# The opening of a fused attention and expert kernel in another order: first inverse ahead of weight conversion, two inverses alternating, chunk 2's scores in earlier slots

## The chip, the cores and the metric

The kernel runs on one core of one Trainium2 chip. The metric is the time of one execution on the device, in microseconds (us). The version before took 1119.66 us (median of 3 runs, 1117.63 to 1121.74).

## The reference: what is computed

Three layers, one behind the other, on 4 batches of 768 positions. The first is a recurrence over positions with a 40 x 40 state for each of 8 heads, the second a gated projection, the third a choice of one expert of 8 for each token.

```python
for t in range(S):                       # attention: B=4, H=8, S=768, D=40
    y[:, :, t] = r_t @ state
    Sa = state @ a_t
    state = state * w_t - outer(Sa, b_t) + outer(v_t, k_t)
...
x = ((x @ w_a) * (x @ w_b)) @ w_out      # 3072 x 320 -> 1536 -> 320
...
expert = argmax(x @ w_gate)              # 8 experts
out = gate * (relu(x @ w1[expert]) @ w2[expert])
```

## The kernel before

The recurrence is worked in 12 chunks of 64 positions. Inside a chunk it becomes matrix products, once a small triangular system is solved. For each chunk the kernel

- loads the decays w, the rows a, b, k and r, and scans w along the chunk (L558 to L563, VectorE), scales b and k by the scan (L601, VectorE) and a by w (L574, GpSimd);
- spreads a and r over the heads (`ablk`, `rblk`, L578, ScalarE), takes the scores as matrix products (L611) and copies them out of PSUM (L619); GpSimd masks them (L621), and SyncE sends them to a scratch tensor `nd` in DRAM (L628);
- reloads them as `m` (L677, L679), one system of 32 x 32 in each partition, and inverts it in `tinv` on VectorE: 31 steps, each one multiplication (L686, `tmp<-m,xt`) and one subtraction (L692, `xt<-xt,tmp`). `xt` starts as the identity, which is loaded (L680). A step reads what the step before wrote;
- sends `xt` to DRAM (`td`, L703) and back in another layout (`s`, L707, L708), transposes and multiplies it there (`forward`: L725, L729, L736, L748, L752), and uses it with the values (`vn`, `pu`, L810) and the state (L821 to L913) for the chunk's result.

`phase1` runs over the chunks c = 0 to 11, each in 24 slots. Tables say what each slot issues: `FIRST` for c = 0 and 1, `STEADY` and `LAST` for the others. With chunk c run matrix products of the gated projection of chunk c-1 (L1071), parts of the inverse of chunk c+1, and the scans, spreads and scores of chunk c+2.

In c = 0 and 1 the kernel also turns the projection weights from 32-bit words of two bit fields into pairs of an upper and a lower TensorE operand: `split64`, of 30 pieces and 4 steps a piece that `conv.take` hands out. A piece takes four VectorE operations on the raw words (L420, L424, L433, L435; tiles `c_f`, `c_s`), some three to six on ScalarE (L422, L430, L432, L443) and two or three on GpSimd (L438, L440, L445). The raw words come by DMA (L972 to L975), some pieces ahead. Pieces are named by their part of the weights: `raw_0_2` is the one with L443 on ScalarE and L440 on GpSimd, where GpSimd must have ended before ScalarE's L443. The tiles c_f have 3 buffers, c_s 2.

Ahead of the loop stands the opening: scans for chunks 0 and 1, scores of both, chunk 0's inverse, a first part of chunk 1's, and the first conversion steps. `mix` lays lists of operations beside one another in even proportion. The order of operations on TensorE, VectorE, ScalarE and GpSimd is the order of the code; each of these engines goes through it strictly. SyncE only issues DMAs; their order is made by the scheduler from the code's order and each DMA's needs. SyncE too takes them one after another, and one that must wait holds those behind it.

Touched by the change are `phase1` (the opening and the loop's use of the tables), the table `FIRST`, the scores, `tinv`, a new `load_x`, and the loading ahead in `split64`.

Of the kernel before, what the change touches and what calls it, by code (L numbers as in the profile page):

```python
# [8 lines left out]
F32 = mybir.dt.float32  # L9
# [13 lines left out]
R = C // 2  # L23
# [108 lines left out]

def phase1(tc, I, cst, drm, psA, psM, ident, hT, mk_ident, wo, xs, span, tiny, down):
    nc = tc.nc
# [3 lines left out]
    A = Attention(tc, I, att, mid, cst, drm, psA, ident, dv, ot, span)  # L138
    A.sink, M.pc = M, A.p2

    def run(fs):
        for f in fs:
            f()

    conv = M.weight_steps()
# [27 lines left out]
    for pr in range(2):  # L173
        A.scale_a(0, pr)
        A.spread_a(0, pr)
    A.ones()
    M.ahead()
    for b in range(B):
        A.scores(0, b)
# [4 lines left out]
        A.rows(0, b)  # L184
    tinv = A.tinv(0)
    for pr in range(2):
        A.vload(0, pr)
        A.load_r(0, pr)
    for pr in range(2):
        A.scale_a(1, pr)  # L190
        A.spread_a(1, pr)
    n0, n1, n2, n3 = FIRST["conv0"]
    run(conv.take(n0))
    for b in range(B):
        A.scores(1, b)
    for b in range(B):
# [2 lines left out]
    uh = [view(M.p2.tile([128, 2, 256], F32, tag="uh", name=f"m1_{h}")) for h in range(2)]  # L199
    xt = M.p2.tile([128, 2, 256], F32, tag="wo", name="xt1", bufs=1)  # L200
    t1 = A.tinv(1, (uh, view(xt)))
    run(conv.take(n1))
    A.relayout(0)
    A.relayout(1)
    mix(tinv, conv.take(n2))
    A.load_w(2)
    for h in range(2):
        A.load_bk(2, h)
    lead = FIRST["lead"]
    mix(t1[:lead], [lambda: A.forward((0, 0))] + conv.take(n3))  # L210
    t1 = t1[lead:]
    over = [A.spans(0, [t[:120, 0:L // 2].bitcast(F32) for t in sp])]
    units, tinv = [], t1
    for c in range(NCH + 1):
# [149 lines left out]
    if not down:  # L364
# [25 lines left out]
        [], [("stage4", 0, 1)], [("stage2v", 2, 3)], [],  # L390
        [("stage5", 0, 1), ("stage3", 2, 3)], [], [("px", 1, 0)],
        [("stage4", 2, 3)], [], [], [("stage5", 2, 3)], [], [], [], []],
    "conv0": [8, 6, 10, 8], "lead": 16, "early": 13, "extra": [10, 17], "ones": [2, 14],
    "conv": [
# [6 lines left out]
    "load_a": [19, 21], "r00": [2, 3, 4], "r1": [8, 9, 10], "score": [15, 16, 17, 18], "row": [16, 17, 22, 23],  # L401
    "tinv": [4, 4, 4, 4, 4, 4, 4, 4, 4, 4, 4, 2, 0, 0, 0, 0, 0, 0, 0, 0, 0, 0, 0, 0], "relayout": 14, "load_w": 15,
    "span": 18, "scan": [21, 22, 22, 23, 23],
}

# [54 lines left out]
class Attention:  # L460
# [144 lines left out]
    def scores(self, c, b):  # L605
        nc = self.nc
        st = self.st[c]
        ps = self.ps.tile([128, 512], F32, tag="pa", name=f"s1p{c}_{b}")
        for g in range(3):
            n = 3 if g < 2 else 2  # L610
            nc.tensor.matmul(  # L611
                ps[:2 * C, 3 * g * C:(3 * g + n) * C], self.bk5(c, b, g),
                self.ablk[b // 2][:, b % 2, g, 0:n, 0:C], start=True, stop=True)
        pr = b // 2
        if b % 2 == 0:
            st["s1"][pr] = self.p2.tile([128, 2, 8, C], F32, tag=f"s1_{pr}", name=f"s1_{c}_{pr}")
        s1p = st["s1"][pr]
        s1 = s1p[:, b % 2]
        nc.scalar.copy(s1, ps.rearrange("p (h t) -> p h t", t=C))  # L619
        v = s1[vrows(b)]  # L620
        nc.gpsimd.affine_select(  # L621
            out=v, in_=v, pattern=[[0, 8], [1, C]], base=0,
            channel_multiplier=-1, compare_op=ALU.is_gt, fill=0.0)
        def send():
            for k in range(2):
                for x in range(2):
                    s = 16 * pr + 8 * x
                    nc.sync.dma_start(  # L628
                        st["nd"][k, s:s + 8].rearrange("s j t -> j s t"),
                        s1p[urow(x, R * k), x, :, R * k:R * k + R])  # L630
# [19 lines left out]
    def relayout(self, c):  # L650
# [6 lines left out]
        for k, p0, p1, g, q0 in (  # L657
            (0, 0, 120, 0, 0), (0, 120, 128, 1, 0), (1, 0, 112, 1, 8), (1, 112, 128, 2, 0),
            (2, 0, 64, 2, 16), (2, 64, 128, 2, 16)):
            nc.sync.dma_start(gp[p0:p1, k, :, 0:C], v[q0:q0 + p1 - p0, :, g, :])  # L660

    def tinv(self, c, room=None):


        nc = self.nc
        st = self.st[c]
        if room:
            m, xt = room
        else:
            t = self.p1.tile([128, R, R], F32, tag="m", name=f"m{c}")  # L670
            m = [t[:, R // 2 * h:R // 2 * h + R // 2] for h in range(2)]
            xt = self.p1.tile([128, R // 2, R], F32, tag="xt", name=f"xt{c}")
        for k in range(2):
            for q in range(2):
                p = slice(64 * k + 32 * q, 64 * k + 32 * q + 32)
                for h in range(2 if room else 0):
                    nc.sync.dma_start(m[h][p], st["nd"][k, :, R // 2 * h:R // 2 * h + R // 2])  # L677
                if not room:
                    nc.sync.dma_start(t[p], st["nd"][k])  # L679
        nc.sync.dma_start(xt, self.I["one"].rearrange("p (i t) -> p i t", t=R))  # L680

        def mul(s, box):
            n, rows = R - 1 - s, s // 2 + 1
            tmp = self.p2.tile([128, 136], F32, tag="tmp", name=f"tmp{c}_{s}")[:, :rows * n]
            box.append(tmp.rearrange("p (i t) -> p i t", t=n))
            nc.vector.tensor_tensor(  # L686
                box[0], m[2 * s // R][:, s % (R // 2):s % (R // 2) + 1, s + 1:].to_broadcast([128, rows, n]),
                xt[:, :rows, s:s + 1].to_broadcast([128, rows, n]), op=ALU.mult)

        def sub(s, box):  # L690
            rows = s // 2 + 1
            nc.vector.tensor_tensor(  # L692
                xt[:, :rows, s + 1:], xt[:, :rows, s + 1:], box[0], op=ALU.subtract)
# [224 lines left out]
class MoeUp:  # L918
# [31 lines left out]
    def weight_steps(self):  # L950
# [10 lines left out]
        def load(j):  # L961
            if j in raws or j >= len(pieces):
                return
            f, q, k = pieces[j]
            f2 = slice(2 * f, 2 * f + 2 * n)
            pool, tag = (self.p2, ("xh", "xl")[j % 2]) if self.early else (self.pc, "raw")
            if self.extra and not self.early and j % 2:
                raw = raws[j] = self.extra[j // 2 % 2]
            else:
                raw = raws[j] = pool.tile([128, 2 * n], I32, tag=tag, name=f"raw{f}_{q}_{k}")  # L970
            if k < 2:
                nc.sync.dma_start(raw, ws[q][128 * k:128 * k + 128, f2])  # L972
            else:
                nc.sync.dma_start(raw[lo], ws[0][256:320, f2])
                nc.sync.dma_start(raw[hi], ws[1][256:320, f2])  # L975

        self.ahead = lambda: [load(j) for j in range(3)]

        def step(j):
            f, q, k = pieces[j]  # L980
            fs = slice(f, f + n)
            for d in range(3 if self.early or self.extra else 2):
                load(j + d)
            raw = raws[j]
# [849 lines left out]
```

## Time and profile before

| what | us |
| --- | --- |
| median of 3 runs | 1119.66 |
| the profiled execution, its own time | 1117.87 |
| its span, from the first to the last instruction | 1115.7 |
| TensorE busy in the span | 984.3 (88%) |
| VectorE busy | 698.4 (63%) |
| ScalarE busy | 590.9 (53%) |
| GpSimd busy | 428.6 (38%) |

The profiled execution lies 1.79 us under the median; 2.2 us of its time lie outside the span. Its mean granted TensorE clock is 0.942 of full speed.

The profile names the engines PE (matrix products) and PEld (weight loads) of TensorE, DVE (VectorE), ACT (ScalarE), POOL (GpSimd) and SP (SyncE; SPq is its queue of DMA issues). The opening takes the stretch from 0 to about 62 us of the span, the loop's c = 0 that from 62 to 135, c = 1 from 135 to 202, c = 2 from 202 to about 253.

### The profile page before, as it was taken

The page shows a single profiled execution, that of the slowest core. Times are in us where ns is not written, and L with a number is a line of the kernel's source. Part 1 is how long each engine was busy: PE and PEld are TensorE (multiplying, and loading weights), DVE is VectorE, ACT ScalarE, POOL GpSimd, SP SyncE. Part 2 cuts the span into 40 slices and gives each one's busy share as a digit, 9 for nine tenths or more (in the row PEclk, how much of TensorE's full clock was granted, in tenths as well). Part 3 has the DMA queues.
Part 4 walks back from the last instruction along what each step waited for, and adds up shares of the span by engine and source line. Part 5 has one row for each costly group of instructions (what it writes and reads, how often), then busy time and mean ns, then how long its engine had stood idle before and what let it go on. Part 6 is the DMA issues. An engine that isn't in the chain of part 4 may idle for free.

```text
span 1115.7 us, 27103 instructions
## 1 busy us (share of the span) xinstructions
PE 984.3 (88%) x10402; PEld 941.8 (84%) x10402; DVE 698.4 (63%) x1843; ACT 590.9 (53%) x1373; POOL 428.6 (38%) x469
## 2 busy tenths in 40 slices
PE   4054587999999999999999999999999999999994
PEld 4054487999898989899899999999998899999994
DVE  7889689686886969697875821336667732222230
ACT  5357867566666666566665553323334354444430
POOL 4326555233423334343232123002224467666641
PEclk9556689899999999999999999979999999999997
DMA  8553343476758576575756124715567264444500
GB/s 206 154 154 87 100 127 100 129 152 161 144 153 175 139 169 150 134 159 148 148 139 137 55 75 113 225 60 179 165 181 235 92 216 141 142 147 141 161 17 16
DMA packets 200663, 154.10 MB, mean 138 GB/s; under 512 B 107269, under 2 KB 182630, under 8 KB 200524
## 3 DMA queue, kind: packets, MB, share of 16 engines
q1 hardware_dynamic: 187196, 132.91, 45.2%
q0 software_dynamic: 9808, 15.76, 5.9%
q10 hardware_dynamic: 3520, 3.61, 1.2%
q8 instruction: 84, 1.38, 0.5%
q14 instruction: 55, 0.45, 0.2%
HBM read 103.66 MB, written 44.60 MB: 133 GB/s over the span
## 4 chain that ended last, share of the span: by engine, by line
PE 58%; DVE 18%; DMA 8%; issue 5%; ACT 4%; POOL 3%; SPq 1%; POOLq 0%; DVEq 0%; ACTq 0%
PE pm L1071 18%; PE py L1208 9%; PE dn L1517 6%; PE u L1497 6%; DVE tmp L686 3%; DVE xt L692 3%; PE s1p L611 3%; PE p L871 2%; DMA out<-y,ids 2%; PE pp L855 1%; PE py L895 1%; PE ta L729 1%; PE px L800 1%; PE tb L748 1%; DVE suf L559 1%
## 5 line engine op out<-in xcount | busy, mean ns | idle before, releaser
L878 POOL TENSOR_SCALAR_AFFINE_SELECT s<-s 64x512 f32<-64x512 f32 x96 | 75.9, 790 | 169.0 <-ACT s L876 164.8
L686 DVE TENSOR_TENSOR tmp<-m,xt 128x126 f32<-128x126 f32 (+22 forms) x372 | 116.4, 313 | 33.1 <-DMA xt<-in_one 14.6
L1071 PE MATMUL pm<-xl,wh 128*128 128x256 f32 x576 | 129.3, 306 | 1.3 <-ACT ua L1074 1.1
L1500 DVE SCALAR_TENSOR_TENSOR hl<-u,hh 128x384 fp32r<-128x384 f32 (+5 forms) x72 | 41.5, 580 | 139.8 <-ACT hh L1499 139.8
L1083 DVE TENSOR_TENSOR uh<-pm,ua 128x256 f32<-128x256 f32 x144 | 60.2, 418 | 105.4 <-PE pm L1071 58.5
L692 DVE TENSOR_TENSOR xt<-xt,tmp 128x126 f32<-128x126 f32 (+22 forms) x372 | 115.9, 311 | 8.6
L1071 PE MATMUL pm<-xh,wl 128*128 128x256 f32 x576 | 116.6, 284 | 0.0
L1071 PE MATMUL pm<-xh,wh 128*128 128x256 f32 x576 | 116.4, 284 | 0.0
L1208 PE MATMUL py<-wh,hl 128*128 128x328 f32 x288 | 91.2, 317 | 2.5 <-DVE hl L1198 2.5
L1208 PE MATMUL py<-wl,hh 128*128 128x328 f32 x288 | 92.2, 320 | 0.6 <-DVE wl L1179 0.6
L1071 PEld LDWEIGHTS pm<-xl,wh 128*128 128x128 f32 x576 | 89.0, 192 | 4.4 <-ACT ua L1074 1.7
L1208 PE MATMUL py<-wh,hh 128*128 128x328 f32 x288 | 90.8, 315 | 0.0
L1071 PEld LDWEIGHTS pm<-xh,wh 128*128 128x128 f32 x576 | 90.5, 193 | 0.0
L1071 PEld LDWEIGHTS pm<-xh,wl 128*128 128x128 f32 x576 | 90.1, 192 | 0.0
L1071 PE MATMUL pm<-xh,w 128*128 128x256 f32 x288 | 82.0, 285 | 0.0
L1071 PE MATMUL pm<-xl,w 128*128 128x256 f32 x288 | 81.9, 284 | 0.0
L1261 POOL DMA_INDIRECT xs<-xr,si x24 | 28.0, 1166 | 137.8 <-DVE acc L1256 88.0
L729 PE MATMUL ta<-t,s 32*32 32x32 f32 x768 | 23.8, 202 | 61.7 <-DVE t L725 58.0
L729 PEld LDWEIGHTS ta<-t,s 32*32 32x32 f32 x768 | 18.8, 116 | 67.3 <-ACT wh L432 32.5
L1050 POOL TENSOR_TENSOR xl<-xf,xh 128x384 fp32r<-128x384 f32 x24 | 24.8, 1034 | 131.5 <-ACT xh L1049 131.5
L1517 PE MATMUL dn<-l,hh 128*128 128x320 f32 (+3 forms) x240 | 74.9, 312 | 0.0
L1517 PE MATMUL dn<-h,hl 128*128 128x320 f32 (+3 forms) x240 | 74.1, 309 | 0.0
(238 smaller groups left out, 2857.6 us busy)
## 6 DMA issues: line engine op xcount, KB each, us to landing
hT<-uh SPq DMA_DIRECT2D x72, 256.0 KB
hf<-hT SPq DMA_DIRECT2D x36, 512.0 KB
r<-in_moe_w SPq DMA_DIRECT2D x8, 1280.0 KB
r<-in_moe_w SPq DMA_DIRECT2D x8, 1024.0 KB
bk<-in_bk SPq DMA_DIRECT2D x22, 360.0 KB
xs<-zt SPq DMA_DIRECT2D x8, 805.0 KB
m<-nd SPq DMA_DIRECT2D x44, 128.0 KB
at<-in_a SPq DMA_DIRECT2D x24, 180.0 KB
```

Of the source, the lines that this page charges most:

```text
L611: nc.tensor.matmul(ps[:2 * C, 3 * g * C:(3 * g + n) * C], self.bk5(c, b, g), self.ablk[b // 2][:, b % 2, g, 0:n, 0:C], start=True, stop=True)
L686: nc.vector.tensor_tensor(box[0], m[2 * s // R][:, s % (R // 2):s % (R // 2) + 1, s + 1:].to_broadcast([128, rows, n]), xt[:, :rows, s:s + ...
L692: nc.vector.tensor_tensor(xt[:, :rows, s + 1:], xt[:, :rows, s + 1:], box[0], op=ALU.subtract)
L729: nc.tensor.matmul(pa[b % 2][urow(b, R), R * h:R * h + R], s1[b % 2][urow(b, 0), h, R:C], t11[urow(b, 0), h, :], start=True, stop=True)
L878: nc.gpsimd.affine_select(out=s2t[q * C:q * C + C], in_=s2t[q * C:q * C + C], pattern=[[0, 8], [1, C]], base=0, channel_multiplier=-1, com ...
L1071: nc.tensor.matmul(p, l, r, start=(i == 0), stop=(i == len(seq) - 1))
L1083: nc.vector.tensor_tensor(h[:, f % 2], p, a, op=ALU.mult)
L1208: self.nc.tensor.matmul(py, self.pair[i][l][:, k, s], self.W[r][:, first + k, cols], start=(first + k == 0 and n == 0), stop=(first + k == ...
L1261: self.nc.gpsimd.indirect_dma_start(self.xs[:], bass.IndirectOffsetOnAxis(ap=si[:, i:i + 1], axis=0), xr[:, j, :], None, bounds_check=NE * ...
L1497: nc.tensor.matmul(p, l, r, start=(i == 0), stop=(i == len(seq) - 1))
L1500: nc.vector.scalar_tensor_tensor(out=hl, in0=p, scalar=0.0, in1=hh.bitcast(F32), op0=ALU.max, op1=ALU.subtract)
L1517: nc.tensor.matmul(p, l[:, q], r[:, f], start=(f == 0 and i == 0), stop=(f == len(hs) - 1 and i == 2))
```

## The change

The totals of work stay as they are; only the order moves, and two buffers' loads.

- **Opening.** Before, 14 operations of conversion stood ahead of chunk 0's inverse on VectorE, the inverse ran mixed with ten conversion steps, and then came 16 operations of chunk 1's inverse with eight conversion steps. Now chunk 0's inverse comes first: 34 of its 62 operations mixed with 16 conversion steps, the other 28 alternating with the first 28 operations of chunk 1's inverse, then six more of that with `forward` and four conversion steps.
- **Loads.** The identity for chunk 0 is issued ahead of the weights (`load_x`); four raw pieces instead of three are issued ahead, and the early lookahead is four pieces. The relayouts, and chunk 2's loads of w, b and k, stand behind chunk 0's inverse in the code.
- **Table FIRST.** The rest of chunk 1's inverse is in slots 0 to 5 of c = 0 instead of 0 to 11; conversion takes three steps a slot instead of two in slots 0 to 11; chunk 2's spans, scans, b and k, a, spreads and scores move up by four or five slots. The mask of chunk 2's scores is issued three slots later than their copy.

```diff
@@ opening
+    A.load_x(0)
     M.ahead()
...
     tinv = A.tinv(0)
     for pr in range(2):
-        A.vload(0, pr)
-        A.load_r(0, pr)
-    for pr in range(2):
         A.scale_a(1, pr)
         A.spread_a(1, pr)
-    n0, n1, n2, n3 = FIRST["conv0"]
-    run(conv.take(n0))
...
     t1 = A.tinv(1, (uh, view(xt)))
-    run(conv.take(n1))
+    n0, n1 = FIRST["conv0"]
+    lead = FIRST["lead"]
+    mix(tinv[:lead], conv.take(n0))
+    k = len(tinv) - lead
+    mix(tinv[lead:], t1[:k])
+    for pr in range(2):
+        A.vload(0, pr)
+        A.load_r(0, pr)
     A.relayout(0)
     A.relayout(1)
-    mix(tinv, conv.take(n2))
     A.load_w(2)
     for h in range(2):
         A.load_bk(2, h)
-    lead = FIRST["lead"]
-    mix(t1[:lead], [lambda: A.forward((0, 0))] + conv.take(n3))
-    t1 = t1[lead:]
+    mix(t1[k:k + 6], [lambda: A.forward((0, 0))] + conv.take(n1))
+    t1 = t1[k + 6:]
@@ FIRST
-    "conv0": [8, 6, 10, 8], "lead": 16,
+    "conv0": [16, 4], "lead": 34,
-    "span2": 4, "scan2": 9, "bk": [12, 13], "sa": [12, 13], "score": [15, 16, 17, 18],
+    "span2": 0, "scan2": 4, "bk": [7, 8], "sa": [7, 8], "score": [11, 12, 14, 14],
-    "tinv": [4, 4, 4, 4, 4, 4, 4, 4, 4, 4, 4, 2, 0, ...
+    "tinv": [8, 8, 4, 4, 4, 4, 0, 0, 0, 0, 0, 0, 0, ...
@@ scores
+        if c == 2:
+            self.ot.later(3, mask)
+        else:
+            mask()
@@ split64
-        self.ahead = lambda: [load(j) for j in range(3)]
+        self.ahead = lambda: [load(j) for j in range(4)]
-            for d in range(3 if self.early or self.extra else 2):
+            for d in range(4 if self.early else 3 if self.extra else 2):
```

In what follows the lines of the changed kernel are some 11 lines further on than those of the kernel before (the inverse is L697 and L703 there, conversion L421 to L446). Numbers behind a tile's name tell buffers apart.

VectorE where the opening's last scaling (L601) ends, before: `m_242` is chunk 0's system.

```order
L601 TENSOR_TENSOR wh_r<-wh_r,suf_207 120x6x64 x4
L420 TENSOR_SCALAR c_f<-raw_0_0_167 128x256
L424 SCALAR_TENSOR_TENSOR c_f<-raw_0_0_167,c_f 128x256
...
L424 SCALAR_TENSOR_TENSOR c_f<-raw_1_1_278,c_f 128x256
L686 TENSOR_TENSOR tmp_0_402<-m_242,xt_243 128x31
L692 TENSOR_TENSOR xt_243<-xt_243,tmp_0_402 128x31
L686 TENSOR_TENSOR tmp_1_405<-m_242,xt_243 128x30
```

The same place now, and behind it the start of the alternation: `m_246` and `xt_167` are chunk 0's, `m_0_317` and `xt_319` chunk 1's.

```order
L602 TENSOR_TENSOR wh_r<-wh_r,suf_211 120x6x64 x4
L697 TENSOR_TENSOR tmp_0_329<-m_246,xt_167 128x31
L421 TENSOR_SCALAR c_f<-raw_0_0_169 128x256
L703 TENSOR_TENSOR xt_167<-xt_167,tmp_0_329 128x31
...
L697 TENSOR_TENSOR tmp_17_437<-m_246,xt_167 128x126
L697 TENSOR_TENSOR tmp_0_439<-m_0_317,xt_319 128x31
L703 TENSOR_TENSOR xt_167<-xt_167,tmp_17_437 128x9x14
L703 TENSOR_TENSOR xt_319<-xt_319,tmp_0_439 128x31
```

The 14 conversion operations between the scaling and the inverse have gone behind the inverse's first operations, and from its 35th operation on the two inverses take turns.

SyncE around the load of chunk 2's w (`w_545`), before:

```order
L660 DMA gp_395<-w_r 64x4x64 x2
L972 DMA raw_0_1_432<-in_moe_w_a 128x512
L972 DMA raw_1_0_500<-in_moe_w_b 128x512
L514 DMA w_545<-in_w 120x781
L520 DMA bk_0_548<-in_bk 120x768
L520 DMA bk_1_550<-in_bk 120x768
L703 DMA td_0_103<-xt_243 512x1x32 x2
L703 DMA td_0_104<-xt_243 512x1x32 x2
```

Now (`w_555`), with ScalarE's first use of it behind, in the second fence of the two:

```order
L714 DMA td_0_103<-xt_167 512x1x32 x2
L714 DMA td_0_104<-xt_167 512x1x32 x2
...
L719 DMA s_0_1_198<-td_0_104 32x8x64
L666 DMA gp_541<-w_113 64x4x64 x2
L666 DMA gp_548<-w_r 120x4x64
...
L666 DMA gp_548<-w_r 64x4x64 x2
L515 DMA w_555<-in_w 120x781
L521 DMA bk_0_558<-in_bk 120x768
```

```order
L747 ACTIVATE pt_0_633<-ta_1_616 32x256
L444 CAST w_0_590<-c_f 64x256
L444 CAST w_0_591<-c_f 64x256
L423 ACTIVATE c_k<-raw_0_0_385 128x256
L538 ACTIVATE junk,span<-w_555,wlim 120x384 x2
L763 COPY s_0_0_181<-tb_0_667 32x8x32
L763 COPY s_0_0_181<-tb_1_668 32x8x32
L747 ACTIVATE pt_1_708<-ta_2_690 32x256
```

The load of w stood ahead of the inverse's way through DRAM, and stands behind it and behind the relayouts gp now; its first reader on ScalarE (L538, then L537) has moved from behind the copies L752 of both halves of `s` to ahead of the first.

GpSimd around the masking of chunk 0's `s` (L878), before, `w_0_434` and `w_0_435` being the upper operands of a `raw_0_2` piece:

```order
L438 TENSOR_TENSOR c_f<-c_f,w_0_434 64x256
L438 TENSOR_TENSOR c_f<-c_f,w_0_435 64x256
L440 TENSOR_TENSOR c_f<-c_f,c_s 128x256
L878 AFFINE_SELECT s_0_0_927<-s_0_0_927 64x512 x2
L878 AFFINE_SELECT s_0_1_931<-s_0_1_931 64x512 x2
L438 TENSOR_TENSOR c_f<-c_f,wh_0_265 128x256
```

The same place now:

```order
L446 TENSOR_TENSOR wl_108<-c_f,c_s 128x256
L889 AFFINE_SELECT s_0_0_958<-s_0_0_958 64x512 x2
L889 AFFINE_SELECT s_0_1_962<-s_0_1_962 64x512 x2
L575 TENSOR_TENSOR at_0_636<-at_0_636,w_555 120x384
L439 TENSOR_TENSOR c_f<-c_f,w_0_590 64x256
L439 TENSOR_TENSOR c_f<-c_f,w_0_591 64x256
L441 TENSOR_TENSOR c_f<-c_f,c_s 128x256
```

The `raw_0_2` piece's three operations have moved from ahead of the four maskings to behind them and behind one scaling of chunk 2's a.

## Rows read from the trace of the kernel before

**Rows 1.** Busy time by stretch: stretch, length, five engines, PE clock, DMA share, GB/s.

```profile
62.00:135.00 73.00, 40.52 (x466) 36.97 (x467) 57.06 (x127) 53.73 (x147) 37.55 (x48) 0.64 0.45 118
135.00:202.00 67.00, 55.36 (x663) 51.44 (x662) 57.42 (x139) 45.39 (x122) 34.05 (x39) 0.86 0.48 125
202.00:253.00 51.00, 49.18 (x686) 46.82 (x686) 40.58 (x109) 33.17 (x83) 15.47 (x22) 1.00 0.58 124
```

**Rows 2.** Waits of DVE, 62 to 135: line, releaser, us in all, times, longest.

```profile
DVE c_s L433 <- POOL wl L445: 10.7, 3, 5.2
```

**Rows 3.** Timeline, 17 to 32: start, duration, engine, line, tiles, idle before.

```profile
17.11 5.04 DVE L601 TENSOR_TENSOR wh_r<-wh_r,suf 120x384 f32<-120x384 f32 x4
20.88 3.15 ACT L578 ACTIVATE ablk<-at,bd 120x384 f32<-120x384 f32 x6 [0.44 <-POOL at L574]
20.91 1.75 SPq L679 DMA_DIRECT2D m<-nd  x4
31.88 0.71 DVE L686 TENSOR_TENSOR tmp<-m,xt 128x31 f32<-128x31 f32 x1
```

**Rows 4.** Timeline of DVE, 39 to 56: inverse steps and a conversion step among them.

```profile
39.41 0.28 DVE L686 TENSOR_TENSOR tmp<-m,xt 128x110 f32<-128x110 f32 x1
39.72 0.27 DVE L692 TENSOR_TENSOR xt<-xt,tmp 128x110 f32<-128x110 f32 x1
...
43.25 0.78 DVE L692 TENSOR_TENSOR xt<-xt,tmp 128x136 f32<-128x136 f32 x1
...
55.55 0.19 DVE L686 TENSOR_TENSOR tmp<-m,xt 128x30 f32<-128x30 f32 x1
55.66 0.42 DVE L435 SCALAR_TENSOR_TENSOR c_s<-raw,c_s 128x256 f32<-128x256 uint32 x1
```

**Rows 5.** Timeline of SP's issues, 42 to 64.

```profile
42.15 4.46 SPq L660 DMA_DIRECT2D gp<-w_r  x6
...
55.23 2.64 SPq L703 DMA_DIRECT2D td<-xt  x4
...
62.68 0.45 SPq L708 DMA_DIRECT2D s<-td  x1
```

**Rows 6.** Timeline, chunk 0's w: its issue, and its first reader.

```profile
0.81 0.48 SPq L514 DMA_DIRECT2D w<-in_w  x1
```

```profile
4.38 0.56 DVE L558 TENSOR_SCALAR w<-w 120x768 f32<-120x768 f32 x1 [4.38 <-DMA w<-in_w]
```

**Rows 7.** Timeline of ACT, 67 to 89.

```profile
67.75 0.75 ACT L752 COPY s<-tb 32x256 f32<-32x256 f32 x2
...
83.40 0.61 ACT L537 ACTIVATE junk<-w,wlim 120x384 bf16<-120x384 f32 x1
...
85.01 0.82 ACT L443 CAST w<-c_f 64x256 fp32r<-64x256 f32 x2
...
88.32 1.06 ACT L876 COPY s<-p 128x512 f32<-128x512 f32 x2
```

**Rows 8.** Timeline of POOL, 78 to 101.

```profile
78.97 1.79 POOL L438 TENSOR_TENSOR c_f<-c_f,w 64x256 f32<-64x256 f32 x2 [5.62 <-DVE xt L692]
80.84 0.72 POOL L440 TENSOR_TENSOR c_f<-c_f,c_s 128x256 f32<-128x256 f32 x1
88.97 3.98 POOL L878 TENSOR_SCALAR_AFFINE_SELECT s<-s 64x512 f32<-64x512 f32 x4 [7.40 <-ACT s L876]
...
99.43 1.20 POOL L574 TENSOR_TENSOR at<-at,w 120x384 f32<-120x384 f32 x1
```

**Rows 9.** Busy time by stretch, as rows 1, from the copies to pt.

```profile
89.28:134.73 45.45, 20.03 (x199) 18.43 (x200) 33.76 (x58) 33.87 (x94) 31.30 (x39) 0.68 0.39 93
```

**Rows 10.** Waits of ACT in that stretch, as rows 2.

```profile
ACT s L619 <- PE s1p L611: 2.6, 2, 1.7
ACT w L443 <- POOL c_f L440: 2.6, 2, 1.8
...
ACT ablk L578 <- POOL at L574: 1.3, 1, 1.3
```

More of the change, by code (lines that the diff above doesn't have):

```diff
@@ L392 @@
         [("stage4", 2, 3)], [], [], [("stage5", 2, 3)], [], [], [], []],
-    "conv0": [8, 6, 10, 8], "lead": 16, "early": 13, "extra": [10, 17], "ones": [2, 14],
+    "conv0": [16, 4], "lead": 34, "early": 13, "extra": [10, 17], "ones": [2, 14],
     "conv": [
[1 row of a table removed]
[1 row of a table added]
         3, 3, 3, 3, 3, 3, 3, 3, 4, 4, 3, 3],
@@ L399 @@
         2, 1, 2, 1, 2, 1, 2, 1, 2, 2, 1, 1],
[1 row of a table removed]
-    "load_a": [19, 21], "r00": [2, 3, 4], "r1": [8, 9, 10], "score": [15, 16, 17, 18], "row": [16, 17, 22, 23],
-    "tinv": [4, 4, 4, 4, 4, 4, 4, 4, 4, 4, 4, 2, 0, 0, 0, 0, 0, 0, 0, 0, 0, 0, 0, 0], "relayout": 14, "load_w": 15,
[1 row of a table added]
+    "load_a": [19, 21], "r00": [2, 3, 4], "r1": [8, 9, 10], "score": [11, 12, 14, 14], "row": [12, 17, 22, 23],
+    "tinv": [8, 8, 4, 4, 4, 4, 0, 0, 0, 0, 0, 0, 0, 0, 0, 0, 0, 0, 0, 0, 0, 0, 0, 0], "relayout": 14, "load_w": 15,
     "span": 18, "scan": [21, 22, 22, 23, 23],
@@ L620, in scores @@
         v = s1[vrows(b)]
-        nc.gpsimd.affine_select(
+        mask = lambda: nc.gpsimd.affine_select(
             out=v, in_=v, pattern=[[0, 8], [1, C]], base=0,
             channel_multiplier=-1, compare_op=ALU.is_gt, fill=0.0)
+        if c == 2:
+            self.ot.later(3, mask)
+        else:
+            mask()
         def send():
@@ L660, in relayout, with load_x @@
             nc.sync.dma_start(gp[p0:p1, k, :, 0:C], v[q0:q0 + p1 - p0, :, g, :])
+    def load_x(self, c):
+        xt = self.of(c)["xt"] = self.p1.tile([128, R // 2, R], F32, tag="xt", name=f"xt{c}")
+        self.nc.sync.dma_start(xt, self.I["one"].rearrange("p (i t) -> p i t", t=R))
     def tinv(self, c, room=None):
@@ L671, in tinv @@
             m = [t[:, R // 2 * h:R // 2 * h + R // 2] for h in range(2)]
-            xt = self.p1.tile([128, R // 2, R], F32, tag="xt", name=f"xt{c}")
+            xt = st["xt"] if c == 0 else self.p1.tile([128, R // 2, R], F32, tag="xt", name=f"xt{c}")
         for k in range(2):
@@ L679, in tinv @@
                     nc.sync.dma_start(t[p], st["nd"][k])
-        nc.sync.dma_start(xt, self.I["one"].rearrange("p (i t) -> p i t", t=R))
+        if c:
+            nc.sync.dma_start(xt, self.I["one"].rearrange("p (i t) -> p i t", t=R))
         def mul(s, box):
```

4 rows, old and new, of the table FIRST are left out of this document.

## The prediction

> **What bounds the kernel now.** I read the busy time by stretch first. From 202 us on, PE is busy 49.18 of 51 us [rows 1]; whatever comes before 202 moves the end of the run one for one, and nothing after it gives time back. Engines' orders are the same again in the second half of c = 0, so the question is by how much the boundary between c = 0 and c = 1 moves (134.73 us, where the stretch of rows 9 ends; "the seam" below). In 62 to 135 PE is busy 40.52 of 73 us, DVE 57.06, ACT 53.73, POOL 37.55 [rows 1]: DVE and ACT are both near full, no single engine fills the stretch. Then the waits: DVE's largest is for POOL's lower operands, 10.7 us in three waits [rows 2]. Then the timelines of each engine at the places that the orders show as changed. In c = 1 DVE is busy 57.42 of 67 us [rows 1]; the work there is the same in both kernels, so I let it shift along with the seam.
>
> **Inverse 0's start.** With the conversion gone, DVE has nothing between the end of L601 at 22.15 [rows 3] and the landing of `m`. SP issued m's four loads from 20.91 on [rows 3]. In the new order they stand behind the first send of chunk 1's scores, which needs ACT's six `ablk` (20.88 to 24.03) [rows 3] and then the scores and their copy, about 0.6 us: 24.6. The send, then 1.75 us of m's issues [rows 3], ends at about 26.8; with some 2 us to land, an estimate, the inverse begins at 28.8, against 31.88 [rows 3]. So 14 conversion operations leave this place and the start gains only 3.1 us: 6.6 us of DVE stand empty.
>
> **Inverse 0's end.** Dependent steps follow each other at 0.31 us (39.41 to 39.72) [rows 4], the narrow first and last ones faster; I take 0.295. 34 steps: 10.0 us. An independent conversion step between them begins before the step ahead has ended (55.55 lasts 0.19, the next begins at 55.66) [rows 4], and so costs 0.10 to 0.23, not its 0.29 to 0.42; 16 of them: 2.6 us. Steps that fall beside a POOL operation take 0.78 instead of about 0.3 [rows 4]; eight of these: 3.8 us. The last 28 operations alternate with 28 of inverse 1. By the same overlap a step costs its 0.25 less 0.09: 0.16 x 56 = 9.0 us. Sum 28.8 + 10.0 + 2.6 + 3.8 + 9.0 = 54.2, against 55.23 where SP sends the inverse [rows 5]. Inverse 0 gains 1 us, and 28 operations of inverse 1 are done by then. All of the 6.6 us that stood empty is won back by the alternation.
>
> The trace shows overlap between independent operations (0.08 us) and none between dependent ones [rows 4]. The Trainium skill, "VectorE: DVE Perf Modes", section "The DRAIN you can't avoid", says that the next operation doesn't start until the pipe has emptied, and that chaining without semaphores skips none of it (it adds that one which isn't held starts earlier). By the first half of that, alternation saves nothing; that is rival D below.
>
> **Chunk 2's w comes late.** This is the term that decides. SP's load of w stood ahead of `td`; now it stands behind td and s, two sends of gp and six more. td to the end of s took 55.23 to 63.13 [rows 5], 7.9 us; two gp at 0.7 (4.46 / 6) make 1.4 and six 4.46 [rows 5]. The load is issued at 54.2 + 7.9 + 1.4 + 4.5 = 68.0. The first w landed 3.57 us after the start of its issue (0.81 to 4.38) [rows 6]: 71.6. ACT's first span on w now stands ahead of the copies of s. ACT's rows ahead of it (pt, the first piece's casts, one square) are done by about 65.5, an estimate from inverse 0's end plus the way that the copies of s took before (55.23 to 67.75) [rows 5, 7] less their last step on PE; so it idles 6 us, and the two spans (0.61 each and some 0.1 for the sum) [rows 7] push the copies from 67.75 [rows 7] to 73.0: 5.2 us later. Of that, 1.5 us of spans and 0.8 us of L443 [rows 7] no longer stand between these copies and L876, and 0.6 us goes where PE's answers came later than ACT anyway: L876 is at about 90.2 instead of 88.32 [rows 7], 1.9 us late. The lower bound is nothing, if SP's sends are quicker than before; the upper the full 5.2.
>
> **POOL behind the masks.** POOL's four masks (3.98) [rows 8] follow L876's first copy: 90.8 to 94.8; then the scaling of a (1.20), L438 (1.79) and L440 (0.72) [rows 8] end at 98.5. Before, these two stood ahead of the masks and ended at 81.56 [rows 8], and L443 on ACT found them done [rows 7]. Now ACT reaches it at about 92.7 and waits 5.8 us; it ends at 98.5 + 0.8 = 99.3. DVE waits too, since the tile c_s of that piece isn't free, about 5 us; what is queued behind on DVE is conversion for c = 0's later slots.
>
> **From there to the seam.** In 89.28 to 134.73 ACT is busy 33.87 us [rows 9] and idles 11.6. From 99.3 on, it has the same work and one piece of conversion more (three steps a slot instead of two; 1.1 us, L422 and the casts): 35.0. If it never waited, the seam would be at 134.3, 0.4 us earlier than now: the floor. With all of its waits as before, 145.9, 11.2 us later. Chunk 2's scores now come four slots earlier, so I take away the waits on the scores (2.6), on a (1.3) and on POOL's c_f (2.6) [rows 10], 6.5 in all; 5.1 remain. Seam: 99.3 + 35.0 + 5.1 = 139.4, **4.7 us later**.
>
> **Edits that I put at nothing.** The identity ahead of the weights and the fourth raw piece change when 3 to 4 loads are issued in the first 30 us; there `m` ends the wait, not they. Were a raw piece late, the conversion step that waits for it would hold the inverse's steps behind it on DVE, by less than the 3.57 us of a whole load [rows 6]. The mask three slots later: POOL then works while PE goes on; its cover is that m of chunk 2 is needed only in c = 1, and without it a few tenths. `forward` is started earlier by a us: ahead of ACT's wait, so worth nothing.
>
> **The forecast.** The profiled execution, 1117.87 us, would be 1122.6; it lies 1.79 us under the median. On the median: 1119.66 + 4.7 = 1124.4, said as 1124.5.
>
> **Rivals.**
>
> *A, faster: chunk 2's w is there in time.* If the load lands by the time that ACT reaches its span, at about 65.5, the copies of s are not held, L876 stands at its old place or ahead, and POOL's detour costs only what it takes itself. For it: inverse 1 is through some 19 us earlier, and DVE's 10.7 us of waits [rows 2] lie in a part of c = 0 where the new order has scores and conversion earlier. Against it: six us of SP's issues would have to go. Price: ACT's L443 then isn't waited for, and ACT's 35.0 us of work begin at 89.3: 124.3 without waits, 129.4 with 5.1: the seam 5.3 us earlier, 1114.4 on the median, at best 1109.2. It decides from the moment that w lands, with the border at 66 us.
>
> *B, no difference: ACT's floor.* All the places above come as I have them, but the waits that remain on ACT shrink to one or two us, since everything is issued earlier than it is needed. The seam lies at -0.4 to +2: 1119.3 to 1121.7, with 1120.5 in the middle.
>
> *C, slower still: nothing of the early scores helps.* The waits of rows 10 stay at 11.6 us, other work in their places: 1119.66 + 11.2 = 1130.9.
>
> *D, no overlap on DVE.* Alternating steps then cost 0.28 each, 56 x 0.28 = 15.7 instead of 9.0 us: inverse 0 ends at 60.9, and everything behind it comes 6.7 us later: 1131.1. The overlap of conversion steps [rows 4] is against it.
>
> **How the numbers follow.** The forecast (seam +2.5 to +7) has 0.42, A 0.22, B 0.22, C 0.09, D 0.05. A measurement of this kernel can tell about 0.3%, 3.4 us, from no change: same is 1116.3 to 1123.0. The forecast's lower end (1122.2 to 1123) gives same 0.07 of its chance, and of A's 0.22 0.02 falls above 1116.3. Faster 0.20, same 0.31 (0.22 + 0.07 + 0.02), slower 0.49. The range takes in the forecast, B, most of A and the lower part of C: 1113 to 1130. It leaves out A's best end (0.05), the upper half of C (0.06) and D (0.05). The forecast's own range is 1122 to 1127.
>
> **What would show it.** Right: the first L697 on DVE at 28 to 30; two inverses' steps at about 0.16 us a step between 42 and 54; w's issue on SP at about 68 and ACT's wait for w of 4 to 6 us ahead of L763; ACT's L444 waiting for POOL's L441 near 93 to 99; the t, pt pair of chunk 1 near 139. Wrong: w issued ahead of td or landed by 66; inverse 0's end above 58; ACT waiting for PE's scores again; or a shift that c = 1 gives back, so that PE's dense stretch begins at 202 in spite of a late seam.

## The result, and the profile after

The changed kernel takes 1127.58 us (median of 7 runs, 1122.97 to 1131.87) against 1120.32 us of the kernel before (7 runs, 1116.66 to 1122.83). The medians lie 7.3 us apart; the ratio on record is 1.0077, 95% interval 1.0050 to 1.0104: slower by 0.8%, some 8.6 us. Forecast were 1124.5 us, 4.8 over the median known then, in a range from 1113 to 1130; the forecast's own narrower range, 1122 to 1127, ends 0.6 us under the measured median.

The profiled execution after took 1126.61 us, its span 1124.6. Its busy time by stretch (columns as in rows 1; the last stretch runs from the end of ACT's L444 to the seam):

```profile
62.00:135.00 73.00, 33.73 (x407) 30.33 (x403) 46.66 (x104) 52.14 (x146) 36.03 (x47) 0.64 0.54 138
135.00:202.00 67.00, 51.76 (x642) 48.10 (x642) 60.87 (x146) 46.34 (x127) 34.58 (x42) 0.85 0.40 105
202.00:253.00 51.00, 47.81 (x631) 45.64 (x630) 38.55 (x102) 32.26 (x79) 17.34 (x23) 0.93 0.65 143
100.90:142.57 41.67, 13.77 (x157) 12.59 (x157) 22.50 (x44) 34.45 (x97) 25.01 (x35) 0.62 0.50 129
```

Beside [rows 1], DVE was busy 46.66 us instead of 57.06 in 62 to 135, PE 33.73 instead of 40.52: less got done there, and no engine was nearer to full; the engines waited more. The timeline of ACT shows for what, and where the seam went: to 142.57, 7.8 us later than 134.73.

```profile
72.17 0.61 ACT L538 ACTIVATE junk<-w,wlim 120x384 bf16<-120x384 f32 x1 [7.80 <-DMA w<-in_w]
...
73.64 0.75 ACT L763 COPY s<-tb 32x256 f32<-32x256 f32 x2
...
92.42 1.05 ACT L887 COPY s<-p 128x512 f32<-128x512 f32 x2
...
100.06 0.83 ACT L444 CAST w<-c_f 64x256 fp32r<-64x256 f32 x2 [6.58 <-POOL c_f L441]
...
124.00 0.83 ACT L444 CAST w<-c_f 64x256 fp32r<-64x256 f32 x2 [3.90 <-POOL c_f L441]
...
142.57 0.78 ACT L747 ACTIVATE pt<-ta 32x256 f32<-32x256 f32 x2 [0.99 <-PE ta L740]
```

The bracket at a row's end is the idle time ahead of it and who ended it. The first wait comes from SP. Its timeline there, to be read beside [rows 5]:

```profile
45.02 3.74 SPq L666 DMA_DIRECT2D gp<-w  x4
55.26 2.58 SPq L714 DMA_DIRECT2D td<-xt  x4
...
58.09 1.40 SPq L718 DMA_DIRECT2D s<-td  x3
...
61.51 0.45 SPq L719 DMA_DIRECT2D s<-td  x1
62.01 1.65 SPq L666 DMA_DIRECT2D gp<-w  x2
63.70 4.50 SPq L666 DMA_DIRECT2D gp<-w_r  x6
68.31 0.54 SPq L515 DMA_DIRECT2D w<-in_w  x1
```

Between 48.8 and 55.3 SP issued nothing: it stood at td, which waits for inverse 0, with eight sends of gp and all of chunk 2's loads behind. SP's longest wait from 20 to 75 (line, releaser, us in all, times, longest):

```profile
SPq L714 <- DVE tmp L697: 7.0, 1, 7.0
```

The second and third wait come from POOL, whose timeline shows four masks, and the piece that ACT wants behind them, twice:

```profile
93.06 3.30 POOL L889 TENSOR_SCALAR_AFFINE_SELECT s<-s 64x512 f32<-64x512 f32 x4 [0.84 <-ACT s L887]
96.44 0.98 POOL L575 TENSOR_TENSOR at<-at,w 120x384 f32<-120x384 f32 x1
97.39 1.77 POOL L439 TENSOR_TENSOR c_f<-c_f,w 64x256 f32<-64x256 f32 x2
99.24 0.79 POOL L441 TENSOR_TENSOR c_f<-c_f,c_s 128x256 f32<-128x256 f32 x1
...
117.73 2.86 POOL L889 TENSOR_SCALAR_AFFINE_SELECT s<-s 64x512 f32<-64x512 f32 x4
...
121.65 1.52 POOL L439 TENSOR_TENSOR c_f<-c_f,w 64x256 f32<-64x256 f32 x2
123.24 0.72 POOL L441 TENSOR_TENSOR c_f<-c_f,c_s 128x256 f32<-128x256 f32 x1
```

The part that was meant to win did what it says. DVE's timeline has the start, one pair of alternating steps in the middle, and the last pair, with the end of inverse 0:

```profile
29.77 0.19 DVE L697 TENSOR_TENSOR tmp<-m,xt 128x31 f32<-128x31 f32 x1 [7.43 <-DMA m<-nd]
...
47.47 0.41 DVE L697 TENSOR_TENSOR tmp<-m,xt 128x120 f32<-128x120 f32 x2
47.80 0.40 DVE L703 TENSOR_TENSOR xt<-xt,tmp 128x120 f32<-128x120 f32 x2
...
55.05 0.41 DVE L703 TENSOR_TENSOR xt<-xt,tmp 128x16 f32<-128x16 f32 x2
```

Two steps of two inverses take 0.33 us from start to start (47.47 to 47.80), where one step alone took 0.31 [rows 4].

### The profile page after: what moved, and what is told of

It is laid out like the page before. It is cut to its first block, busy times and chain, and to the rows that moved or that the text cites. A ratio compares the mean times of both kernels' runs of the same rounds, so it can differ in the third digit from the quotient of the medians.

```text
span 1124.6 us, 27089 instructions
## 1 busy us (share of the span) xinstructions
PE 981.9 (87%) x10402; PEld 940.4 (84%) x10402; DVE 689.8 (61%) x1843; ACT 590.5 (53%) x1373; POOL 425.6 (38%) x469
## 5 line engine op out<-in xcount | busy, mean ns | idle before, releaser
L889 POOL TENSOR_SCALAR_AFFINE_SELECT s<-s 64x512 f32<-64x512 f32 x96 | 73.3, 764 | 164.0 <-ACT s L887 159.8
L697 DVE TENSOR_TENSOR tmp<-m,xt 128x126 f32<-128x126 f32 (+22 forms) x372 | 111.2, 302 | 34.1 <-DMA xt<-in_one 16.1
L703 DVE TENSOR_TENSOR xt<-xt,tmp 128x126 f32<-128x126 f32 (+22 forms) x372 | 114.6, 311 | 8.0
L1082 PEld LDWEIGHTS pm<-xh,wl 128*128 128x128 f32 x576 | 90.6, 193 | 0.0
L1528 PE MATMUL dn<-h,hh 128*128 128x320 f32 (+3 forms) x240 | 74.1, 309 | 0.0
L1085 ACT COPY ua<-pm 128x256 f32<-128x256 f32 x144 | 53.3, 370 | 36.9 <-PE pm L1082 34.6
```

The costliest lines, as they stand in the source:

```text
L697: nc.vector.tensor_tensor(box[0], m[2 * s // R][:, s % (R // 2):s % (R // 2) + 1, s + 1:].to_broadcast([128, rows, n]), xt[:, :rows, s:s + ...
L703: nc.vector.tensor_tensor(xt[:, :rows, s + 1:], xt[:, :rows, s + 1:], box[0], op=ALU.subtract)
L889: nc.gpsimd.affine_select(out=s2t[q * C:q * C + C], in_=s2t[q * C:q * C + C], pattern=[[0, 8], [1, C]], base=0, channel_multiplier=-1, com ...
L1082: nc.tensor.matmul(p, l, r, start=(i == 0), stop=(i == len(seq) - 1))
L1085: nc.scalar.copy(a, p)
L1528: nc.tensor.matmul(p, l[:, q], r[:, f], start=(f == 0 and i == 0), stop=(f == len(hs) - 1 and i == 2))
```

## The experiments

Two causes were put to the test, SP's queue and POOL's order, and two rivals: that ACT and DVE are simply full, and that the alternation itself crowds DVE. The table has each kernel's ratio to the kernel before and its seam, which is the start of ACT's pt of chunk 1 in the profiled execution. Each ratio is to runs of the kernel before taken with it. By the ratio, the time moved in all of them by what the seam moved, to within 1.5 us. The identity and the fourth raw piece, which the prediction put at nothing, stand in all of these kernels but the kernel before and e7, so what they are worth alone was not tried.

| kernel | what differs | ratio (95% interval) | seam, us |
| --- | --- | --- | --- |
| before | | 1 | 134.7 |
| changed | | 1.0077 (1.0050 to 1.0104) | 142.6 |
| e8 | changed, without chunk 2's new slots | 1.0094 (1.0078 to 1.0111) | 143.7 |
| e7 | before, with chunk 2's new slots alone | 1.0003 (0.9984 to 1.0023) | 134.2 |
| e5 | changed, no alternation | 1.0080 (1.0051 to 1.0109) | 143.5 |
| e2 | changed, spans on w later | 1.0067 (1.0045 to 1.0088) | 142.4 |
| e1 | changed, loads ahead of the alternation | 1.0049 (1.0029 to 1.0068) | 139.7 |
| e3 | changed, the first piece ahead of the masks | 1.0041 (1.0015 to 1.0067) | 140.0 |
| e4 | e1 and e3 | 1.0021 (0.9999 to 1.0042) | 136.9 |
| e10 | changed, loads ahead of inverse 0 | 1.0002 (0.9986 to 1.0018) | 135.6 |
| e6 | e10, and both pieces ahead of the masks | 0.9972 (0.9954 to 0.9990) | 131.2 |
| e9 | e6, and ten conversion steps ahead of inverse 0 | 0.9953 (0.9935 to 0.9972) | 130.5 |
| e11 | e9, no alternation | 0.9993 (0.9976 to 1.0010) | 135.1 |

**Which part costs: e7 and e8.** Each has one half of the change. The edit of e7, made in the kernel before (with the mask as in the change), which e8 makes backwards in the changed kernel:

```diff
-    "span2": 4, "scan2": 9, "bk": [12, 13], "sa": [12, 13], "sp": [[13, 14, 15], [14, 15, 16]],
+    "span2": 0, "scan2": 4, "bk": [7, 8], "sa": [7, 8], "sp": [[8, 9, 10], [9, 10, 11]],
-    "score": [15, 16, 17, 18], "row": [16, 17, 22, 23],
+    "score": [11, 12, 14, 14], "row": [12, 17, 22, 23],
```

> The kernel before with one part of the change alone: chunk 2's spans, scan, scalings, spreads, scores and rows in the new slots, and the mask three slots later. The opening, conversion and inverse tables stay. Theory 1: w is there early in this kernel, so the early spans wait for nothing; the waits on chunk 2's scores leave c = 0, and the seam comes 0 to 4 us earlier than 134.7; the time 0 to 3 us under the kernel before's. Rival: the early scores themselves crowd ACT and POOL in front of the masks of s: seam 3 us and more later, time 3 us and more over.

> The other part alone: the changed kernel with chunk 2's spans, scan, scalings, spreads, scores, rows and mask back in the slots of the kernel before. Theory 1: w is late and the masks stand ahead of the conversion piece as in the changed kernel, and the waits on chunk 2's scores are back as well: the seam at 141 to 146, the time 5 to 10 us over the kernel before's. Rival (the loss comes from the early scores): the seam near 134.7, the time within 2 us of the kernel before's.

The earlier scores alone are worth nothing that the runs can tell (1.0003), the opening with its conversion table is the whole loss (1.0094). In e7 the waits on the scores went, but POOL's turned up elsewhere; ACT's longest waits in 62 to 135 (line, releaser, us in all, times, longest):

```profile
ACT ablk L578 <- POOL at L574: 4.9, 1, 4.9
ACT w L443 <- POOL c_f L440: 4.6, 2, 3.9
```

In e8 ACT waited 6.49 us for POOL's L441 as in the changed kernel. At the seam theory 1 held on both sides (134.2 and 143.7); the time of e8, some 10.5 us over by its ratio, lies a little above the 5 to 10 expected.

**SP's queue: e1, e2 and e10.** In e1 the block of relayouts and loads stands between the two `mix` calls, in e10 ahead of both; e2 leaves it and puts the spans back. The edit shows where the lines come in; behind the second `mix` they go.

```diff
@@ e1 (e10: ahead of "n0, n1 = FIRST[...]")
     mix(tinv[:lead], conv.take(n0))
+    for pr in range(2):
+        A.vload(0, pr)
+        A.load_r(0, pr)
+    A.relayout(0)
+    A.relayout(1)
+    A.load_w(2)
+    for h in range(2):
+        A.load_bk(2, h)
...
@@ e2
-    "span2": 0,
+    "span2": 4,
```

> The changed kernel, but the relayouts and chunk 2's loads of w, b and k stand ahead of the alternating part of the inverses, so SyncE issues w before it waits for the inverse, not behind it. Theory 1 (two delays add up: the late w holds ACT's copies of s, then POOL's masks hold ACT's L444): w lands by about 58, ACT never waits for it, L887 at 86 to 88 instead of 92.4, the seam (ACT's pt of chunk 1, 142.6 in the changed kernel) at 137 to 138, the time 5 us under the changed kernel's, about 1122. Rival 2 (ACT and DVE are full from 62 to the seam, so an earlier start is eaten up by other waits): the seam within 1.5 us of 142.6, the time unchanged. Rival 3 (alternating inverses and the early rest of inverse 1 crowd DVE): seam unchanged too, and L697 and L703 stay the reason for waits.

> The changed kernel with chunk 2's spans on w back in slot 4 of c = 0 instead of slot 0; w is as late as before, but on ACT its first reader stands behind the copies of s. Theory 1: ACT's wait of 7.8 us at the span goes, the copies of s come at about 67; DVE's scan of w and what hangs on it stay where they are (78). L887 at 88 to 90, the seam at 138 to 139.5, the time 3 to 4.5 us under the changed kernel's. Rival 2: within 1.5 us. If e1 gains and this doesn't, it is the scan of w and not the span on ACT that costs.

> The changed kernel with the relayouts and chunk 2's loads ahead of inverse 0 in the code, as in e6, but with its own conversion table, so that the masks still stand ahead of the pieces with L444. Theory (SP's queue and POOL's order are two causes, each worth half): the seam between that of the changed kernel, 142.6, and that of e6, 131.2: 136 to 138; ACT's waits for L441 9 to 11 us; the time 0.2 to 0.5% over the kernel before's. If the seam is under 133, POOL's order costs nothing once SP is in time.

e2 missed. The span no longer waited for w, the copies of s came at 63.4 instead of 73.6, and next to nothing was won: L887 came at 91.67, 0.8 us earlier, and the seam moved by 0.2 us. Two rows of e2 say why, the first of ACT, the second of DVE:

```profile
77.23 0.62 ACT L538 ACTIVATE junk<-sp,wlim 120x384 bf16<-120x384 f32 x1 [5.03 <-DMA sp<-in_w]
```

```profile
76.88 0.30 DVE L421 TENSOR_SCALAR c_f<-raw 128x256 int32<-128x256 int32 x1 [7.24 <-DMA raw<-in_moe_w_b]
```

Not w alone is late. The rows `sp` and the raw pieces stand behind it in SP's queue and come late as well; who leaves out the wait for one meets the next. They also landed slowly: `sp`, issued from 70.50 on, ended ACT's wait at 77.23, and from 70 to 78 the DMA share (the mean busy share of the 16 DMA engines) was 0.86 to 1.07. The expectation had named the scan of w on DVE for this outcome; the rows speak against it, since the scan's first step (L559, 78.25) stood behind the conversion step that had waited for a raw piece. e1 takes the relayouts, w, b and k ahead of td; `sp` and the raw pieces stay behind it, but come some 3 us earlier (`sp` at 67.01 instead of 70.26). It gains 2.9 us at the seam, half of what was expected. The missing half is in its SP rows:

```profile
54.90 0.53 SPq L515 DMA_DIRECT2D w<-in_w  x1
...
56.43 2.68 SPq L714 DMA_DIRECT2D td<-xt  x4
62.69 1.32 SPq L718 DMA_DIRECT2D s<-td  x3
```

From td's last issue (59.1) to the first s it took 3.6 us; in the changed kernel this was 0.25 (57.84 to 58.09). With w, b and k issued in the 1.5 us ahead of td, its sends land later, and ACT's first pt came at 66.70 instead of 62.28. In e10 w, b and k were issued 5 us ahead of td (to 49.57), with four loads of raw words between:

```profile
48.14 0.53 SPq L515 DMA_DIRECT2D w<-in_w  x1
...
54.57 2.65 SPq L714 DMA_DIRECT2D td<-xt  x4
58.59 1.34 SPq L718 DMA_DIRECT2D s<-td  x3
```

Its first pt came at 62.60. It gains 7.0 us at the seam with POOL's wait still there:

```profile
92.59 0.83 ACT L444 CAST w<-c_f 64x256 fp32r<-64x256 f32 x2 [6.54 <-POOL c_f L441]
...
135.61 0.77 ACT L747 ACTIVATE pt<-ta 32x256 f32<-32x256 f32 x2 [1.45 <-PE ta L740]
```

That is 0.4 us ahead of the 136 to 138 expected; the time is that of the kernel before (1.0002), where 0.2 to 0.5% over it was expected. ACT's waits for L441, 10.2 us in all, are as expected.

**POOL's order: e3, e4 and e6.** Two steps of conversion more in the first two slots (e3, e4) put POOL's part of the first waited-for piece ahead of the masks, four more in the first four (e6) that of both. The masks had not moved; the pieces had, since the opening now takes 20 conversion steps instead of 32, and the twelve others are made up for one a slot in slots 0 to 11.

```diff
@@ e3, e4
-        3, 3, 3, 3, 3, 3, 3, 3, 3, 3, 3, 3,
-        3, 3, 3, 3, 3, 3, 3, 3, 4, 4, 3, 3],
+        4, 4, 3, 3, 3, 3, 3, 3, 3, 3, 3, 3,
+        3, 3, 3, 3, 3, 3, 3, 3, 3, 3, 3, 3],
@@ e6
+        4, 4, 4, 4, 3, 3, 3, 3, 3, 3, 3, 3,
+        3, 3, 3, 3, 3, 3, 3, 3, 3, 3, 2, 2],
```

> The changed kernel with conversion four steps in slots 0 and 1 and three in slots 20 and 21 (two steps earlier in between): the piece that ACT waited for 6.58 us at L444 has its POOL operations ahead of the four masks. w is still late. Theory 1: ACT's wait for POOL's L441 falls from 6.6 to under 1.5 us, L887 stays at about 92.5 to 93.5, the seam comes 4 to 6 us earlier, 137 to 138.5; the time 4 to 5.5 us under the changed kernel's. Rival 2: ACT waits elsewhere instead (for DVE's c_f or POOL), the seam within 1.5 us.

> e1 and e3 together. Theory 1: both delays gone, they add: the seam at 131 to 134, 9 to 11 us earlier than in the changed kernel and level with or under the kernel before (134.7); the time 1117 to 1119. Rival 2 (ACT's floor): the seam not under 138, the time about 1123.

> The changed kernel with both delays taken out further: relayouts and chunk 2's loads stand ahead of inverse 0 in the code, so that SyncE issues them at 37 to 50 and they no longer collide with td (as in e1, where the way of the inverse through DRAM took 3.6 us longer), and conversion takes four steps in slots 0 to 3, so that both pieces with L444 have their POOL operations ahead of the masks. Theory 1 (w, the collision and the masks are all that made the change slow): ACT's first pt at 61 to 63, L887 at 86 to 88, ACT's waits for L441 under 3 us in all, the seam at 130 to 133, the time 2 to 4 us under the kernel before's. Rival 2 (a floor of ACT and DVE): the seam at 135 to 137, the time 1 to 2 us over the kernel before's, as e4.

e3 won 2.6 us at the seam instead of 4 to 6. The first wait fell to 1.96 us. On ACT, though, L444 now stands ahead of L887, which came at 95.17 instead of 92.42, later than the 92.5 to 93.5 expected; and in e3 the second piece still stands behind the second set of masks, and that wait grew:

```profile
93.98 0.83 ACT L444 CAST w<-c_f 64x256 fp32r<-64x256 f32 x2 [1.96 <-POOL c_f L441]
...
120.42 0.83 ACT L444 CAST w<-c_f 64x256 fp32r<-64x256 f32 x2 [4.79 <-POOL c_f L441]
```

e4 adds the two gains up (2.9 and 2.6 make 5.5; the seam came 5.7 us earlier), which a floor of ACT and DVE would not allow. Its 136.9 lies above the 131 to 134 expected, since neither part was complete: the collision of e1 and the second wait of e3 are both in it. e6 removes these too:

```profile
62.94 0.78 ACT L747 ACTIVATE pt<-ta 32x256 f32<-32x256 f32 x2 [3.75 <-PE ta L740]
...
87.58 0.83 ACT L444 CAST w<-c_f 64x256 fp32r<-64x256 f32 x2 [1.96 <-POOL c_f L441]
...
110.56 0.83 ACT L444 CAST w<-c_f 64x256 fp32r<-64x256 f32 x2 [0.61 <-POOL c_f L441]
...
131.16 0.78 ACT L747 ACTIVATE pt<-ta 32x256 f32<-32x256 f32 x2
```

The seam is 3.6 us ahead of the kernel before's, and the kernel is faster than it by 0.3% (0.9954 to 0.9990). Two bounds were missed narrowly: L887 came at 89.71 (86 to 88 expected), and ACT's waits for L441 were 3.0 us in all (under 3 expected). The floor as a rival has fallen.

**The alternation: e5, e9 and e11.** e5 and e11 run the rest of inverse 0, and then inverse 1, in a row; e9 fills the 7 us that DVE stood empty ahead of inverse 0.

```diff
@@ e5, e11
-    mix(tinv[lead:], t1[:k])
+    run(tinv[lead:])
+    run(t1[:k])
@@ e9, e11
-    mix(tinv[:lead], conv.take(n0))
+    run(conv.take(10))
+    mix(tinv[:lead], conv.take(n0 - 10))
```

> The changed kernel without the alternation: the last 28 operations of inverse 0 run alone, the 28 of inverse 1 behind them. Theory 1 (alternation costs inverse 0 next to nothing and its gain falls where DVE waits for ACT anyway): inverse 0 ends at 54 to 55 instead of 55.4, DVE spends 8 to 9 us on inverse 1 behind it, conversion and the transposes of s come 4 to 6 us later, but ACT's wait for w at 64 to 72 hides most of that; the seam within 2 us of 142.6, the time within 2.5 us of the changed kernel's. Rival D of the prediction's kind (the overlap on DVE is what wins the opening): the seam 6 us later, the time 5 us and more over the changed kernel's. A rival on the other side, that alternation slows inverse 0: its end over 2 us earlier and the time 2 us lower.

> e6 (loads ahead of inverse 0, conversion pieces ahead of the masks) with the first ten conversion steps on DVE ahead of inverse 0, in the 7 us in which DVE waits for m. Theory: the ten steps fit before m lands (22.2 to 26), the inverse still begins at 29 to 30 and ends 1 to 2 us earlier than in e6 (54.8), at 53 to 54; the seam 1 to 2 us earlier, 129.5 to 130.5; the time 1 us under e6's, 0.997 to 0.995 of the kernel before's. Rival: ACT's and POOL's part of these pieces comes no earlier (ACT copies scores until 28), so nothing but the place of the DVE steps changes, and something else on SP or ACT sets td: the seam within 0.5 us of 131.2.

> e9 (SP's loads early, pieces ahead of the masks, ten conversion steps ahead of inverse 0) without the alternation: the last 28 operations of inverse 0 alone, then 28 of inverse 1. In the changed kernel the alternation was worth nothing, but there ACT waited for w behind it. Theory A (alternation gives DVE some 8 us, and they now show, since nothing else holds ACT): pt 4 us later than in e9 (62.3), the seam 3 to 5 us later, 133.5 to 135.5; the time 3 to 5 us over e9's, as the kernel before's. Theory B (in c = 0 ACT and POOL set the pace, DVE's 8 us fit into its waits): the seam within 1.5 us of 130.5, the time unchanged against e9.

In e5 inverse 0 ended at 53.76 (first row below), and SP sent it at 53.79 instead of 55.26: as e5 also began 0.3 us earlier (29.47), the alternation costs inverse 0 itself some 1.2 us, which theory 1 had put at next to nothing. But DVE had the 28 steps of inverse 1 behind it only at 61.82 instead of 55.49. The pt of e5 came 4.6 us later, and ACT's wait for w was 4.0 us shorter:

```profile
53.58 0.18 DVE L704 TENSOR_TENSOR xt<-xt,tmp 128x16 f32<-128x16 f32 x1
...
66.84 0.78 ACT L748 ACTIVATE pt<-ta 32x256 f32<-32x256 f32 x2 [2.35 <-PE ta L741]
...
72.78 0.61 ACT L539 ACTIVATE junk<-w,wlim 120x384 bf16<-120x384 f32 x1 [3.85 <-DMA w<-in_w]
```

So in the changed kernel the alternation was worth 0.9 us at the seam, nothing in time that the runs can tell. In e9, where neither w nor POOL holds ACT for 2 us at a time, the same edit costs 4.5 us at the seam, e9's first here and e11's second:

```profile
130.52 0.78 ACT L748 ACTIVATE pt<-ta 32x256 f32<-32x256 f32 x2
```

```profile
135.05 0.78 ACT L749 ACTIVATE pt<-ta 32x256 f32<-32x256 f32 x2
```

It costs 0.4% of time: e11's interval (0.9976 to 1.0010) lies above e9's (0.9935 to 0.9972). Theory A held. The ten steps of e9 took DVE from 22.4 to 26.9, with the wait for m cut to 2.57 us, and SP sent inverse 0 at 53.98 instead of 54.79 in e6; the gain at the seam is 0.6 us, under the 1 to 2 expected and near the rival's bound. Its time is 0.2% below e6's, and the intervals overlap: whether the fill is worth anything stays open.

## Why the prediction was right, point by point

The direction, the place and the two main waits came as forecast, the size did not: 4.7 us at the seam were forecast and 7.8 measured. The range held the result because it was 17 us wide and took in a part of rival C, so that the time lies in it says less than the points below.

**Inverse 0's start.** Forecast 28.8, measured 29.77; m's issue stood behind the first send of chunk 1's scores as read from the order (25.41), and DVE stood empty for 7.43 us instead of 6.6. From the end of m's issues (27.18) to the first step it took 2.6 us, where 2 had been put in as an estimate.

**Inverse 0's end.** Forecast 54.2, measured 55.26 at SP's td. The 34 steps with conversion took 15.9 us (29.77 to 45.68) against 16.4 summed up; the 56 alternating ones 9.8 us (45.68 to 55.46) against 9.0, 0.175 each. Rival D, by which they would take 0.28 each, is refuted here by the rows and not by the time. It rests on what the Trainium skill ("VectorE: DVE Perf Modes", "The DRAIN you can't avoid") says first, that the next operation does not start until the pipe has emptied; the 0.175 us a step do not bear that out for these pairs, and agree with its addition, that one which isn't held starts earlier.

**Chunk 2's w.** Issue forecast at 68.0, measured 68.31; landing at 71.6, ACT's wait ended at 72.17; wait 6 us forecast, 7.80 measured; the copies of s at 73.0 against 73.64. L876 (L887 now) was forecast at 90.2 and came at 92.42: I had given back 3.3 of the 5.2 us on the way there, and 1.8 came back. The three terms that I named for it add up to 2.9 and not to 3.3 (1.5, 0.8 and 0.6), so by my own sum L876 belonged at 90.6. This term was named as the one that decides, and as a place it was; as a cause it was too narrow. The prediction priced the wait at the span on w; e2 showed that without this wait the loads behind w cost the same.

**POOL behind the masks.** L441's end was forecast at 98.5, measured 100.03, ACT's wait at 5.8, measured 6.58. The masks took 3.30 instead of 3.98.

**From there to the seam.** This is the mis-sized term. Forecast were 35.0 us of work and 5.1 of waits from 99.3 on; measured 34.45 of work and 7.2 of waits, from 100.9 on. The work was right. Of the waits I had taken away POOL's c_f (2.6 in two waits [rows 10]), because chunk 2's scores come earlier. That was wrong: in the kernel before the second set of masks already stands ahead of a piece that ACT waits for, and chunk 2's scores come only behind it. Its rows, of POOL and then of ACT:

```profile
103.45 3.27 POOL L878 TENSOR_SCALAR_AFFINE_SELECT s<-s 64x512 f32<-64x512 f32 x4
...
107.93 1.65 POOL L438 TENSOR_TENSOR c_f<-c_f,w 64x256 f32<-64x256 f32 x2
```

```profile
110.41 0.83 ACT L443 CAST w<-c_f 64x256 fp32r<-64x256 f32 x2 [1.83 <-POOL c_f L440]
...
132.49 0.83 ACT L443 CAST w<-c_f 64x256 fp32r<-64x256 f32 x2 [0.74 <-POOL c_f L440]
```

These two waits stayed: the first grew from 1.83 to 3.90, the other was 0.79 instead of 0.74 (at 139.37). From the start of the masks to the piece's L443 it took 6.96 us before and takes 6.27 now, but ACT reached the piece 5.1 us after that start before and 2.4 us after it now: what ACT no longer waited for ahead of it, it waited for here. I had walked POOL's order through the first set of masks and not through the second. The seam came at 142.57 instead of 139.4: 1.6 us from the later L444, and 1.6 us behind it (2.1 more of waits, 0.5 less of work).

**Behind the seam.** The shift was passed on as forecast. PE's products ta behind ACT's `vn` near 208, before and after:

```profile
207.55 0.69 PE L729 MATMUL ta<-t,s 32*32 32x32 f32 x30 [0.34 <-ACT vn L810]
```

```profile
216.01 0.69 PE L740 MATMUL ta<-t,s 32*32 32x32 f32 x30 [0.34 <-ACT vn L821]
```

8.5 us later, where the seam was 7.8 later, and the two profiled executions differ by 8.7. Nothing in c = 1 gave time back.

**The rivals.** A was forecast to win 5.3 us if w is there by 66 and ACT's L443 then doesn't wait. e10 issues w at 48.14, ahead of td, and still waits 6.54 us at that place: the one doesn't follow from the other. The masks follow ACT's L887 and the piece follows the masks, so all three come earlier together. With both, e6 won 3.6 us at the seam. B (the waits shrink) and C (they stay at 11.6) were both off: after L444 they were 7.2.

## What to carry to other kernels

When a change moves loads behind a DMA that waits for a computation, price the whole queue behind it, not the first reader: every load behind shares the delay, and taking the first reader away only shows the next. Follow each in-order engine through all repetitions of a pattern, since the wait behind the second set of masks, which the sum left out, cost 3.9 us. And judge a local gain (here the alternation) in a version in which nothing later hides it: worth 0.9 us at the seam in the changed kernel, it was worth 4.5 once loads and masks were put in order.

## What the runs showed of the hardware

Loads issued just ahead of a small transfer delayed its landing by over 3 us (3.6 against 0.25 us of wait for td from td's last issue to the first s, with w, b and k in the 1.5 us ahead); with w, b and k issued 5 us ahead and four loads of raw words between, in e10, the wait was 1.4 us (57.22 to 58.59). The DMA share goes with it: 1.05 from 57 to 62 in e1 and 1.02 from 50 to 58 in e10, where the first s followed 0.6 to 0.7 us behind, but 0.47 from 56 to 60 in the changed kernel. So in e1 and e10 the first s went only when the 16 DMA engines were no longer full. Whether the queue or the memory sets the order there was not tried.

Two independent chains of steps on DVE took 0.175 us a step when they alternated, against 0.31 for dependent ones [rows 4].
